# Recurrent cross-attention and a switch mixture of experts in fp32: each batch's x tokens go through one expert unsorted, with the contraction cut to 256 by states @ w1, and the states' tokens run in column groups of 32

## The chip, the cores and the metric

The kernel runs on one core of a Trainium2 chip. The metric is the time of one execution on the device, in microseconds (us); the median of a few runs is quoted, and one further execution is profiled. PE is TensorE (PEld its weight load), DVE VectorE, ACT ScalarE, POOL GpSimd; SP is the engine that here only issues DMAs.

## What is computed

There are B = 8 batches and H = 8 heads; x has S = 512 positions and state Ns = 32, both with D = 64 per head.

```python
scores = scale * x @ state.T;  a = softmax(scores)       # per batch and head
xread = a @ state                                         # 512 rows: the x tokens
scores2 = scale * state @ x.T; a2 = softmax(scores2)
sread = a2 @ x                                            # 32 rows: the states' tokens
x = concat([xread, sread]).transpose(0, 2, 1, 3).reshape(4352, 512)
logits = x @ w_gate;  expert_idx = argmax(logits);  gate_w = max of softmax(logits)
for e in range(8):                                        # w1[e] 512 x 1024, w2[e] 1024 x 512
    mask = expert_idx == e
    out[mask] = gate_w[mask] * (relu(x[mask] @ w1[e]) @ w2[e])
```

A batch contributes 512 x tokens and 32 states' tokens, 4096 and 256 in all. A row of xread is, head by head, a mixture of that batch's 32 states with the weights a. So for all x tokens of a batch x @ w1 = a @ (states @ w1), and the second form contracts over 8 heads x 32 states = 256 instead of over 512.

## The kernel before

All arithmetic of the heavy matmuls is fp32. The engines' orders come from a scheduler that moves instructions of the program as written; buffers come from rotating pools, so that a load waits until the last reader of its buffer is done.

*Attention*, one batch after another. `load_x` brings x in on SP (four DMAs of 256 KB a batch, three buffers); `transpose_x` turns it on PE through PSUM (`xT`, four copies by `evict`, which alternates between ACT and DVE); `prep_state` turns the states (`stT`) and multiplies them with the gate weights (`gst`, so that logits come from the weights a alone); `scores` puts the scores of four head pairs into `pc`, 64 output columns each, alternately in the lower and the upper half of the array. `read_weights` makes the softmax over the states on DVE (`sx`, in 32 x 32 transposes), with the exponential on ACT and the last multiplication on POOL, into `aT`. `write_weights`, `transpose_write` and `write_rows` do the same in the other direction (`a`, `a2T`, `pw`, `xs`) and write the states' tokens to DRAM (`st_dram`). `read_rows` multiplies the x tokens out (`px`, 256 columns a matmul), copies them into `row`, takes their logits (`pl`), and `route` chooses an expert and a slot for each token and scatters the rows, 128 at a time, to a buffer per expert in DRAM (`xs_dram`). `route_states` does this for 128 states' tokens read back from DRAM.

*Experts.* The tokens are sorted by expert, each expert's padded to tiles of T = 256; JT = 24 tiles always run. `fetch(j)` gathers a tile's rows on POOL and loads the 2 MB of `w1t` and the 2 MB of `w2t` on SP, two buffers each; `x_in` transposes the rows; `up` makes hT with K = 512 (64 records of 128 x 256 a tile), `down` multiplies by w2 with 512 columns a matmul (32 records), scales by the gate (L458) and scatters rows to the output on POOL (L459). Up, the next tile's transposes and down follow each other on PE.

Of the kernel before, what the change touches and what calls it, by code (L numbers as in the profile page):

```python
# [9 lines left out]
FP32 = mybir.dt.float32  # L10
# [18 lines left out]
):  # L29
    nc = tc.nc  # L30
# [32 lines left out]

# [11 lines left out]

# [3 lines left out]
    ebase = const.tile([128, E], FP32)  # L79
    nc.gpsimd.iota(ebase[:], pattern=[[NTOK, E]], base=0, channel_multiplier=0,  # L80
                   allow_small_or_imprecise_dtypes=True)
    base_e = const.tile([128, E], FP32)
    nc.vector.tensor_copy(out=base_e[:], in_=ebase[:])
    jio = const.tile([128, JT], FP32)
    nc.gpsimd.iota(jio[:], pattern=[[1, JT]], base=0, channel_multiplier=0,
                   allow_small_or_imprecise_dtypes=True)
    tri8 = const.tile([128, E, E], FP32)
    for e in range(E):
        nc.vector.tensor_scalar(tri8[:, e, :], rev8[:], float(E - e) - 0.5, None, ALU.is_ge)

# [10 lines left out]
    tok_s = const.tile([128, B // 4], I32)  # L101
    for g in range(B // 4):
        nc.vector.tensor_scalar(tmp_p[:], quad[:], float(SO - NS), iota_p[:, 0:1], ALU.mult, ALU.add)
        nc.vector.tensor_scalar(tok_s[:, g:g + 1], tmp_p[:], float(4 * g * SO + S), None, ALU.add)
# [4 lines left out]
    XB = 6  # L109

    xg_bufs = []
    for i in range(XB):
        xg = const.tile([128, XW], FP32, name=f"xg{i}")
        nc.gpsimd.memset(xg[:], 0.0)
        xg_bufs.append(xg)
# [25 lines left out]
    stT = att.tile([128, B, NPR, 2 * NS], FP32, bufs=1)  # L141
    gst = att.tile([128, B, 2, E], FP32, bufs=1)

# [22 lines left out]
    def transpose_x(b):  # L166
        xT = att.tile([128, NPR, NC, 128], FP32, tag="xT", name="xT")
        for j in range(NPR):
# [3 lines left out]
            evict(xT[:, j], pt[:])  # L172
# [10 lines left out]
    def read_weights(pc):  # L183
# [13 lines left out]
        aT = att.tile([128, 2, NC, 128], FP32, tag="aT", name="aT")  # L197
        nc.vector.transpose(aT[:].rearrange("p g c q -> p (g c q)"), sx[:].rearrange("p b n -> p (b n)"))
        return aT
# [15 lines left out]
    def transpose_write(a2):  # L215

        a2T = att.tile([128, 2, NC, 128], FP32, tag="a2T", name="a2T")
        for g in range(2):
# [90 lines left out]
    def route_states(g4):  # L309
# [4 lines left out]
        for c in range(NDC):  # L314
            nc.tensor.transpose(pt[:, c, :], srow[:, 0, ts(c, 128)], ident[:])
# [193 lines left out]
```

## Time and profile before

| what | us |
|---|---|
| median of 3 runs (898.52 to 899.72) | 899.61 |
| the profiled execution | 899.81 |
| its span, first to last instruction | 898.0 |
| PE busy (93% of the span) | 832.9 |
| DVE busy | 220.4 |
| ACT busy | 90.6 |
| POOL busy | 154.9 |

The profiled execution's time is 1.8 us more than its span. PE was granted 0.962 of its full clock in the mean. The DMA moved 138.03 MB.

### The profile page before, as it was taken

To read this page: it belongs to the slowest core of one execution; us is meant where nothing else is said; L and a number is where in the kernel's file an instruction comes from. 1 tells how busy PE (TensorE), PEld (TensorE's weight loads), DVE (VectorE), ACT (ScalarE), POOL (GpSimd) and SP (SyncE) were. 2 spreads that over 40 slices of the span, in tenths; PEclk is the share of its full clock that TensorE was granted. 3 is DMA by queue.
4 is the path that set the end of the run, shared out by engine and by line. 5 is a ranking of instruction groups with operands and counts; after the bars stand their busy time and mean duration, and the time that the engine had idled before them with its cause. 6 is when DMAs were issued, how large, how long until landed. Compare 5 with 4: busy or idle time off the path is not lost.

```text
span 898.0 us, 8743 instructions
## 1 busy us (share of the span) xinstructions
PE 832.9 (93%) x3452; PEld 565.0 (63%) x3452; DVE 220.4 (25%) x560; ACT 90.6 (10%) x176; POOL 154.9 (17%) x158
## 2 busy tenths in 40 slices
PE   3788898729999999999999999999999999999997
PEld 2375566617667766677666776667666776667764
DVE  4584878531111111111111111111111111111100
ACT  1232232201000000000000000000000000000000
POOL 3022324342001101111111101111011110100000
PEclk9888999666999999999999999999999999999999
DMA  9034542159545455463645536455364544445200
GB/s 164 1 74 121 132 125 93 67 175 386 182 161 203 147 205 176 175 213 112 229 152 210 178 129 227 147 199 162 137 205 159 202 124 162 156 160 199 97 1 0
DMA packets 86904, 138.03 MB, mean 154 GB/s; under 512 B 43214, under 2 KB 43214, under 8 KB 86864
## 3 DMA queue, kind: packets, MB, share of 16 engines
q1 hardware_dynamic: 70912, 109.06, 37.8%
q0 software_dynamic: 10400, 26.83, 7.8%
q10 hardware_dynamic: 5552, 1.59, 1.1%
q8 instruction: 27, 0.44, 0.2%
q14 instruction: 13, 0.11, 0.0%
HBM read 122.75 MB, written 22.05 MB: 161 GB/s over the span
## 4 chain that ended last, share of the span: by engine, by line
issue 65%; POOL 8%; DMA 2%; PE 2%; POOLq 1%; DVE 0%; DVEq 0%
POOL out_dram L459 5%; POOL xg L405 3%; PE ph L442 2%; DMA xg<-xs_dram,grow 1%; DMA w1t<-in_moe_w_dram 1%; POOLq L405 0%; POOLq L459 0%; POOLq L504 0%; DMA xs_dram<-srow,r_sli 0%; DVE ti L430 0%; DVE gw L432 0%; DVEq L430 0%
## 5 line engine op out<-in xcount | busy, mean ns | idle before, releaser
L442 PE MATMUL ph<-fxT,w1t 128*128 128x256 f32 x1536 | 338.4, 381 | 0.1
L455 PE MATMUL py<-w2t,hT 128*128 128x512 f32 x768 | 333.6, 592 | 0.0
L442 PEld LDWEIGHTS ph<-fxT,w1t 128*128 128x128 f32 x1536 | 293.8, 191 | 50.6 <-issue 11.4
L455 PEld LDWEIGHTS py<-w2t,hT 128*128 128x128 f32 x768 | 144.2, 190 | 172.3 <-issue 172.0
L459 POOL DMA_INDIRECT out_dram<-y,ti x48 | 48.4, 1009 | 357.0 <-DVE y L458 324.8
L458 DVE TENSOR_SCALAR y<-py,gw 128x512 f32<-128x512 f32 x48 | 36.1, 751 | 293.5 <-PE py L455 293.5
L405 POOL DMA_INDIRECT xg<-xs_dram,grow x48 | 49.5, 1032 | 247.7 <-PE ptx L427 235.0
L447 ACT ACTIVATE hT<-ph 128x512 f32<-128x512 f32 x48 | 28.7, 597 | 555.1 <-PE ph L442 555.1
L445 DVE TENSOR_SCALAR hT<-ph 128x512 f32<-128x512 f32 x48 | 33.1, 690 | 135.6 <-PE ph L442 135.4
L282 PE MATMUL px<-bd,aT 128*128 128x256 f32 x128 | 39.9, 439 | 11.6 <-DVE row L125 4.5
L430 DVE TENSOR_TENSOR ti<-xg,inv_i 128x1 int32<-128x1 int32 x48 | 6.0, 157 | 168.2 <-DMA out_dram<-y,ti 154.3
L268 POOL DMA_INDIRECT xs_dram<-row,r_sli x32 | 31.9, 996 | 60.2 <-DVE r_sli L265 25.1
L427 PE MATMUL ptx<-ident,xg 128*128 128x128 f32 x192 | 28.2, 290 | 13.8 <-DMA xg<-xs_dram,grow 13.7
L282 PEld LDWEIGHTS px<-bd,aT 128*128 128x128 f32 x128 | 24.4, 212 | 20.7 <-DVE row L125 6.5
L171 PE MATMUL pt<-ident,x_nat 128*128 128x128 f32 x128 | 26.4, 342 | 11.5 <-DMA x_nat<-in_x_dram 6.6
L427 PEld LDWEIGHTS ptx<-ident,xg 128*128 128x128 f32 x192 | 23.8, 149 | 17.9 <-issue 14.2
L171 PEld LDWEIGHTS pt<-ident,x_nat 128*128 128x128 f32 x128 | 18.7, 174 | 18.5 <-issue 7.2
L196 POOL TENSOR_TENSOR sx<-sx,sm 128x1024 f32<-128x1024 f32 x8 | 15.3, 1912 | 68.9 <-ACT xT L123 33.7
L179 PE MATMUL pc<-xT,stT 128*64 128x512 f32 x64 | 24.9, 705 | 0.0
L299 PE MATMUL pw<-x_nat,a2T 128*64 128x128 f32 x256 | 20.6, 318 | 3.1 <-DVE a2T L125 2.6
L123 ACT COPY fxT<-ptx 128x512 f32<-128x512 f32 x24 | 14.0, 585 | 88.9 <-PE ptx L427 86.0
L299 PEld LDWEIGHTS pw<-x_nat,a2T 128*64 128x64 f32 x256 | 17.8, 161 | 4.7 <-DVE a2T L125 2.9
(115 smaller groups left out, 331.4 us busy)
## 6 DMA issues: line engine op xcount, KB each, us to landing
w1t<-in_moe_w_dram SPq DMA_DIRECT2D x24, 2048.0 KB, 9.1
w2t<-in_moe_w_dram SPq DMA_DIRECT2D x24, 2048.0 KB, 10.0
x_nat<-in_x_dram SPq DMA_DIRECT2D x32, 256.0 KB, 4.8
xg<-xs_dram,grow POOLq DMA_INDIRECT x48, 6.9
out_dram<-y,ti POOLq DMA_INDIRECT x48, 3.2
bd<-in_state_dram ACTq DMA_DIRECT2D x8, 64.0 KB, 4.2
st_dram<-xs ACTq DMA_DIRECT2D x32, 16.0 KB, 3.5
xs_dram<-row,r_sli POOLq DMA_INDIRECT x32, 3.8
```

Of the source, the lines that this page charges most:

```text
L171: nc.tensor.transpose(pt[:, c, :], x_nat[b][:, c, ts(j, 2), :], ident[:])
L268: d = nc.gpsimd.indirect_dma_start(out=xs_dram[:], out_offset=bass.IndirectOffsetOnAxis(ap=sli[:, u:u + 1], axis=0), in_=row[:, u, :].bitc ...
L282: nc.tensor.matmul(px[:, ts(g, 256)], lhsT=aT[:, g, c, :], rhs=bd[:, b, g], start=True, stop=True, skip_group_check=True)
L299: nc.tensor.matmul(pw[ts(i, 64), g], lhsT=a2T[:, g, c, ts(i, 64)], rhs=x_nat[b][:, c, ts(2 * g + i, 2), :], start=(c == 0), stop=(c == NC ...
L405: nc.gpsimd.indirect_dma_start(out=xg_bufs[(NH * j + k) % XB][:].bitcast(I32), out_offset=None, in_=xs_dram[:], in_offset=bass.IndirectOff ...
L427: nc.tensor.transpose(pt[:, c, :], xg[:, ts(c, 128)], ident[:])
L442: nc.tensor.matmul(ph[:, i, :], lhsT=w1t[:, c, ts(2 * f2 + i, 128)], rhs=xT[:, c, :], start=(c == 0), stop=(c == NDC - 1), skip_group_chec ...
L445: nc.vector.tensor_scalar(hT[:, ts(f2, 2), :], ph[:], 0.0, None, ALU.max)
L447: nc.scalar.activation(hT[:, ts(f2, 2), :], ph[:], AF.Relu)
L455: nc.tensor.matmul(py[:], lhsT=hT[:, f, ts(k, 128)], rhs=w2t[:, f, :], start=(f == 0), stop=(f == NFC - 1))
L458: nc.vector.tensor_scalar(y[:], py[:], gw[:, k:k + 1], None, ALU.mult)
L459: d = nc.gpsimd.indirect_dma_start(out=out[:], out_offset=bass.IndirectOffsetOnAxis(ap=ti[:, k:k + 1], axis=0), in_=y[:], in_offset=None, ...
```

## The change

*Attention.* `read_rows` goes: x tokens are neither multiplied out nor sorted. What is kept of each batch are the weights `aT` and the states `stT`, for all batches. The copies of xT and of a2T are all ACT's. `logits_x` takes the logits of a batch; `route` works on many token groups at once (batches 0 and 1 after batch 1, all the rest at the end), and `choose` counts a batch's tokens per expert by a matmul with ones and takes the most frequent one as the batch's expert (`eb`). The first two batches' weights are loaded then. Only the states' tokens are sorted, into 16 groups of 32 that each belong to one expert (`ss_dram`, `eg`).

*Experts.* Per batch, `states_w1` multiplies the batch's 256 head-states by its expert's w1 into `G` (eight matmuls with 64 output columns); `up` multiplies G by aT with K = 256 and 512 columns; `down` is as before with 512 columns, and its rows go straight to the output by plain DMAs on SP. The states' tokens run in 4 rounds of four groups: the four groups of a round take 32 output columns each, with four experts' weights streamed past them, which `round_w1` and `round_w2` load in tiles of 1 MB, one DMA of 256 KB for each group, three buffers each. A round's up is laid between the column slices of an even batch's down, its down between those of the next batch's down. At the end, if any x token had another expert than its batch, a loop runs the pairs of batch and expert that are left.

```diff
-            evict(xT[:, j], pt[:])
+            nc.scalar.copy(xT[:, j], pt[:])
...
-            evict(a2T[:, g], pt[:])
+            nc.scalar.copy(a2T[:, g], pt[:])
...
-    def read_rows(b, aT):
...
-        for c in range(NC):
-            px = ps_o.tile([128, DM], FP32, tag="o", name="px")
-            for g in range(2):
-                nc.tensor.matmul(px[:, ts(g, 256)], lhsT=aT[:, g, c, :], rhs=bd[:, b, g],
-                                 start=True, stop=True, skip_group_check=True)
-            evict(row[:, c, 0:DM], px[:])
...
-        route(pl[:], row, tok_x[:, b, :], NC)
...
+    def logits_x(b):
+        pl = ps_s.tile([128, NC, E], FP32, tag="s", name="pl")
+        for c in range(NC):
+            for g in range(2):
+                nc.tensor.matmul(pl[:, c, :], lhsT=aT[:, b, g, ts(c, 128)], rhs=gst[:, b, g, :],
+                                 start=(g == 0), stop=(g == 1), skip_group_check=True)
+        evict(lg[:, ts(b, NC)], pl[:])
...
+    def choose(b0, nb):
...
+        for c in range(NC):
+            nc.tensor.matmul(pr[:], lhsT=ones_b[:], rhs=ohb[:, ds(b0, nb), c, :],
+                             start=(c == 0), stop=(c == NC - 1), skip_group_check=True)
...
+    def expert_of(table, i, engines=(SP,)):
...
+    def load_w1(b, e):
+        w1s[b] = wpool.tile([128, NDC, F], FP32, tag="w1", name="w1t")
+        nc.sync.dma_start(out=w1s[b][:], in_=moe_w1[ds(e, 1)].rearrange("o (c p) f -> p (o c) f", p=128))
+
+    def load_w2(b, e):
+        w2s[b] = wpool.tile([128, NFC, DM], FP32, tag="w2", bufs=2, name="w2t")
+        nc.sync.dma_start(out=w2s[b][:], in_=moe_w2[ds(e, 1)].rearrange("o (c p) f -> p (o c) f", p=128))
 
     def weights(b):
         xT = transpose_x(b)
...
     for b in range(B):
-        aT, (a2, s2) = soft
+        a2, s2 = soft
         if b + 2 < B:
             load_x(b + 2)
         if b + 1 < B:
             soft = weights(b + 1)
         a2T = transpose_write(a2)
         write_rows(b, a2T, s2)
-        read_rows(b, aT)
-        if b == 5:
-            route_states(0)
-    route_states(1)
...
+        logits_x(b)
+        if b == 1:
+            route(0, 2 * NC)
+            choose(0, 2)
+            for i in range(2):
+                e = expert_of(eb, i)
+                if i == 0:
+                    load_w1(0, e)
+                load_w2(i, e)
+    logits_s()
+    route(2 * NC, (B - 2) * NC + NST)
+    choose(2, B - 2)
...
+    left = const.tile([128, 1], FP32)
+    nc.vector.tensor_reduce(left[:], cmx[:, :, 0], AX.X, ALU.add)
+    left_i = const.tile([128, 1], I32)
+    nc.vector.tensor_scalar(left_i[:], left[:], -1.0, float(B * S), ALU.mult, ALU.add)
...
+    def states_w1(w1t, st):
+
+        G = ffn.tile([128, 2, F], FP32, tag="G", bufs=1, name="G")
+        for g in range(2):
+            for k in range(2):
+                pg = ps_h.tile([128, 512], FP32, tag="h", name="pG")
+                for i in range(2):
+                    j = 2 * g + i
+                    nc.tensor.matmul(pg[ts(i, 64), :], lhsT=st[:, j, :], rhs=w1t[:, j, ts(k, 512)],
+                                     start=True, stop=True, skip_group_check=True)
+                evict(G[:, g, ts(k, 512)], pg[:])
+        return G
+
+    def up(G, a, insert=None):
+        hT = [ffn.tile([128, S], FP32, tag="hT", bufs=12, name="hT") for _ in range(NFC)]
+        for f in range(NFC):
+            ph = ps_h.tile([128, S], FP32, tag="h", name="ph")
+            for g in range(2):
+                nc.tensor.matmul(ph[:], lhsT=G[:, g, ts(f, 128)], rhs=a[:, g, :],
+                                 start=(g == 0), stop=(g == 1))
+            relu(hT[f][:], ph[:])
...
+    def down(hT, w2t, store, insert=None):
+        for c in range(NC):
+            py = ps_y.tile([128, DM], FP32, tag="y", name="py")
+            for f in range(NFC):
+                nc.tensor.matmul(py[:], lhsT=hT[f][:, ts(c, 128)], rhs=w2t[:, f, :],
+                                 start=(f == 0), stop=(f == NFC - 1))
+            store(c, py)
+            if insert:
+                insert(c)
...
+    def store_batch(b):
+        rows = out[ds(b * SO, S)].rearrange("(p c) f -> p c f", c=NC)
...
+        def store(c, py):
+            y = ffn.tile([128, DM], FP32, tag="y", bufs=3, name="y")
+            scaled(y[:], py[:], gw[:, NC * b + c, :])
+            no_dep(nc.sync.dma_start(out=rows[:, c], in_=y[:]))
+        return store
...
+    def round_in(r):
+        xg = ffn.tile([128, XW], FP32, tag="xg", name="xg")
+        nc.sync.dma_start(out=xg[:].bitcast(I32), in_=ss_dram[ts(r, 128)])
+        rd[r].update(xg=xg, e=[expert_of(eg, 4 * r + q) for q in range(4)])
...
+    def round_w1(r, k, half):
+        t = ffn.tile([128, 4, 512], FP32, tag="s1", bufs=3, name="s1")
+        for q in range(4):
+            nc.sync.dma_start(out=t[:, q], in_=moe_w1[ds(rd[r]["e"][q], 1), ts(k, 128), ts(half, 512)]
+                              .rearrange("o p f -> p (o f)"))
+        rd[r][1, k, half] = t
...
+    def round_w2(r, f):
+        t = ffn.tile([128, 4, DM], FP32, tag="s2", bufs=3, name="s2")
+        for q in range(4):
+            nc.sync.dma_start(out=t[:, q], in_=moe_w2[ds(rd[r]["e"][q], 1), ts(f, 128), :]
+                              .rearrange("o p f -> p (o f)"))
...
+    def round_x(r):
+        pt = ps_t.tile([128, NDC, 128], FP32, tag="t", name="ptx")
+        for c in range(NDC):
+            nc.tensor.transpose(pt[:, c, :], rd[r]["xg"][:, ts(c, 128)], ident[:])
+        xT = ffn.tile([128, NDC, 128], FP32, tag="sxT", name="sxT")
+        evict(xT[:], pt[:])
...
+    def round_up(r, k):
+        for half in range(2):
+            for q in range(4):
+                nc.tensor.matmul(rd[r]["ph"][half][ts(q, 32), :], lhsT=rd[r]["xT"][:, k, ts(q, 32)],
+                                 rhs=rd[r][1, k, half][:, q, :], start=(k == 0), stop=(k == NDC - 1),
...
+    def round_h(r):
+        h = ffn.tile([128, F], FP32, tag="sh", bufs=1, name="sh")
+        for half in range(2):
+            relu(h[:, ts(half, 512)], rd[r]["ph"][half][:])
...
+        for u in range(2):
+            pt = ps_t.tile([128, 4, 128], FP32, tag="t", name="pth")
+            for i in range(4):
+                nc.tensor.transpose(pt[:, i, :], h[:, ts(4 * u + i, 128)], ident[:])
+            evict(hT[:, ts(u, 4)], pt[:])
...
+    def round_down(r, f):
+        for q in range(4):
+            nc.tensor.matmul(rd[r]["py"][ts(q, 32), :], lhsT=rd[r]["hT"][:, f, ts(q, 32)],
+                             rhs=rd[r][2, f][:, q, :], start=(f == 0), stop=(f == NFC - 1),
...
+    def round_out(r):
+        xg = rd[r]["xg"]
+        y = ffn.tile([128, DM], FP32, tag="y", bufs=3, name="ys")
+        scaled(y[:], rd[r]["py"][:], xg[:, DM:DM + 1])
+        no_dep(nc.gpsimd.indirect_dma_start(
...
+
+    G = states_w1(w1s[0], stT[:, 0])
+    e_next = expert_of(eb, 1)
+    load_w1(1, e_next)
+    round_in(0)
+    hT = up(G, aT[:, 0])
+    for b in range(B):
+        r = b // 2
+        if b % 2 == 0:
+            round_x(r)
+            for k in range(NDC):
+                for half in range(2):
+                    round_w1(r, k, half)
+        else:
+            round_h(r)
+            for f in range(NFC):
+                round_w2(r, f)
+            if r + 1 < NR:
+                round_in(r + 1)
+        if b + 1 < B:
+            G = states_w1(w1s[b + 1], stT[:, b + 1])
+        if b + 2 < B:
+            e = expert_of(eb, b + 2)
+            load_w1(b + 2, e)
+            load_w2(b + 2, e)
+
+        def insert(c):
+            if b % 2 == 0:
+                round_up(r, c)
...
-    def down(j):
...
-        for k in range(NH):
-            py = ps_o.tile([128, DM], FP32, tag="o", name="py")
-            for f in range(NFC):
-                nc.tensor.matmul(py[:], lhsT=hT[:, f, ts(k, 128)], rhs=w2t[:, f, :],
-                                 start=(f == 0), stop=(f == NFC - 1))
...
+                round_down(r, 2 * c)
+                round_down(r, 2 * c + 1)
+        down(hT, w2s[b], store_batch(b), insert)
+        if b % 2:
+            round_out(r)
+        if b + 1 < B:
+            hT = up(G, aT[:, b + 1])
...
+    n_left = nc.values_load(left_i[0:1, 0:1], min_val=0, max_val=B * S,
+                            skip_runtime_bounds_check_because="a count of tokens")
+    with tc.If(n_left > 0):
```

PE in the expert stage before, one tile after another: ph is up, ptx the transposes, py down.

```order
L442 MATMUL ph<-fxT,w1t 128x256 x32
L427 MATMUL ptx<-ident,xg_111 128x128 x4
L427 MATMUL ptx<-ident,xg_113 128x128 x4
L455 MATMUL py<-w2t,hT 128x512 x16
L442 MATMUL ph<-fxT,w1t 128x256 x32
```

Here only the next tile's transposes stand between up and down.

PE in the changed kernel, from up of a batch to the middle of its down, in a batch that carries a round's up (pG is states_w1 of the next batch, pgh the round, the names with s_ its weight tiles).

```order
L460 MATMUL ph<-aT,G 128x512 x16
L511 MATMUL ptx<-ident,xg 128x128 x4
L450 MATMUL pG<-w1t,stT 64x512 x8
L471 MATMUL py<-w2t,hT 128x512 x8
L520 MATMUL pgh<-s_1723,sxT 32x512 x4
L520 MATMUL pgh<-s_1728,sxT 32x512 x4
L471 MATMUL py<-w2t,hT 128x512 x8
L520 MATMUL pgh<-s_1733,sxT 32x512 x4
L520 MATMUL pgh<-s_1738,sxT 32x512 x4
```

Two weight tiles of the round now stand in PE's line between each two column slices of down.

SP before, one tile's weights.

```order
L410 TENSOR_LOAD eidx
L414 ISA
L414 DMA w1t<-in_moe_w_dram 128x4x1024
L416 ISA
L416 DMA w2t<-in_moe_w_dram 128x8x512
```

Nothing else stands in that line between one tile and the next.

SP in the changed kernel, from the second half of a round's last up tile (L497) to the first down tile (L504); L483 stores a column slice of the output.

```order
L497 ISA
L497 DMA s_1345<-in_moe_w_dram 128x512
L497 ISA
L497 DMA s_1345<-in_moe_w_dram 128x512
L310 TENSOR_LOAD eb
L319 ISA
L319 DMA w1t<-in_moe_w_dram 128x4x1024
L323 ISA
L323 DMA w2t<-in_moe_w_dram 128x8x512
L483 DMA out_dram<-y 128x512
L504 ISA
L504 DMA s_1511<-in_moe_w_dram 128x512
```

The loads of the batch after next, a store and the tiles of a round now stand in one line on SP, each behind the wait of the one ahead.

PE in the changed kernel at the end of attention: a_1009 is the last batch's a, pls the states' logits.

```order
L227 MATMUL pt<-ident,a_1009 128x128 x8
L450 MATMUL pG<-w1t,stT 64x512
L238 MATMUL pw<-x_nat,a2T 64x128 x8
L263 MATMUL pt<-ident,srow 128x128 x4
L450 MATMUL pG<-w1t,stT 64x512 x4
L238 MATMUL pw<-x_nat,a2T 64x128 x8
L252 MATMUL pl<-gst,aT 128x8 x8
L450 MATMUL pG<-w1t,stT 64x512
L267 MATMUL pls<-wg,sT 128x8 x4
L263 MATMUL pt<-ident,srow 128x128 x4
L267 MATMUL pls<-wg,sT 128x8 x4
```

Six of the first batch's eight states_w1 matmuls have moved ahead of the states' logits; the other two and the first up stand behind them and behind the counts that follow.

## Rows read from the trace of the kernel before

**Rows 1.** Busy time by stage: us, engine busy (instructions), granted clock, DMA share, GB/s.
```profile
28.60:154.10 125.50, 104.16 (x726) 75.30 (x727) 90.98 (x223) 37.57 (x83) 35.62 (x30) 0.90 0.36 92
154.10:190.10 36.00, 25.90 (x178) 19.96 (x178) 18.00 (x62) 6.86 (x15) 12.53 (x12) 0.79 0.30 100
190.10:210.10 20.00, 6.11 (x23) 3.91 (x24) 8.04 (x48) 1.17 (x2) 11.43 (x12) 0.50 0.75 277
210.10:893.10 683.00, 682.93 (x2475) 457.32 (x2475) 91.43 (x202) 41.53 (x70) 86.54 (x85) 1.00 0.48 166
893.10:898.00 4.90, 0.00 (x0) 0.00 (x0) 0.73 (x1) 0.00 (x0) 0.98 (x1) 0.71 0.01 0
```

**Rows 2.** PE's timeline over one tile: start us, us, instruction, count.
```profile
410.57 13.98 PE L442 MATMUL ph<-fxT,w1t 128*128 128x256 f32 x64
424.38 1.04 PE L427 MATMUL ptx<-ident,xg 128*128 128x128 f32 x8
425.26 13.90 PE L455 MATMUL py<-w2t,hT 128*128 128x512 f32 x32
439.00 6.21 PE L442 MATMUL ph<-fxT,w1t 128*128 128x256 f32 x28
```

**Rows 3.** Groups by shape: count | busy us, mean ns | idle before, releaser.
```profile
L442 PE MATMUL ph<-fxT,w1t 128*128 128x256 f32 x1536 | 338.4, 381 | 0.1
L455 PE MATMUL py<-w2t,hT 128*128 128x512 f32 x768 | 333.6, 592 | 0.0
L123 ACT COPY xT<-pt 128x512 f32<-128x512 f32 x16 | 9.4, 585 | 50.1 <-PE pt L171 47.3 <-DVE xT L125 2.8
```

**Rows 4.** PE's timeline in attention, 64 and 128 output columns.
```profile
105.65 1.97 PE L299 MATMUL pw<-x_nat,a2T 128*64 128x128 f32 x32 [1.37 <-DVE a2T L125]
115.78 1.13 PE L282 MATMUL px<-bd,aT 128*128 128x256 f32 x4
116.97 1.06 PE L179 MATMUL pc<-xT,stT 128*64 128x512 f32 x4
117.87 0.59 PE L179 MATMUL pc<-xT,stT 128*64 128x512 f32 x1
```

**Rows 5.** The instructions on sx (min/median/max, first and last start), DVE's timeline.
```profile
L187 DVE STREAM_TRANSPOSE sx<-pc x8: 1218/1250/1251, 28.6 to 154.1; 128x1024 f32<-128x1024 f32 x8
...
101.44 1.25 DVE L187 STREAM_TRANSPOSE sx<-pc 128x1024 f32<-128x1024 f32 x1 [1.41 <-PE pc L179]
110.62 0.69 DVE L125 COPY row<-px 128x512 f32<-128x512 f32 x1
112.03 1.25 DVE L198 STREAM_TRANSPOSE aT<-sx 128x1024 f32<-128x1024 f32 x1 [0.72 <-POOL sx L196]
118.93 1.25 DVE L187 STREAM_TRANSPOSE sx<-pc 128x1024 f32<-128x1024 f32 x1 [1.58 <-PE pc L179]
```

**Rows 6.** Timeline from the last batch's xs to the first up.
```profile
178.33 0.61 DVE L304 TENSOR_SCALAR xs<-pw,s 128x128 f32<-128x128 f32 x2 [3.31 <-PE pw L299]
186.41 0.65 PE L315 MATMUL pt<-ident,srow 128*128 128x128 f32 x4 [0.59 <-DMA srow<-st_dram]
190.14 0.19 PE L251 MATMUL pr<-r_oh,U 128*128 128x8 bf16 x1 [1.06 <-DVE r_oh L238]
203.01 3.37 PE L427 MATMUL ptx<-ident,xg 128*128 128x128 f32 x12 [12.66 <-DMA xg<-xs_dram,grow]
210.12 16.90 PE L442 MATMUL ph<-fxT,w1t 128*128 128x256 f32 x64
```

**Rows 7.** DMA issues: KB each, median us from issue to landing.
```profile
w2t<-in_moe_w_dram SPq DMA_DIRECT2D x24, 2048.0 KB, 10.0
x_nat<-in_x_dram SPq DMA_DIRECT2D x32, 256.0 KB, 4.8
```

**Rows 8.** Busy time while x loads, and while one w2t loads.
```profile
3.00:13.00 10.00, 4.69 (x16) 3.04 (x16) 7.80 (x20) 1.17 (x2) 5.39 (x6) 1.00 1.38 220
245.00:249.00 4.00, 4.00 (x20) 3.51 (x19) 0.00 (x0) 0.00 (x0) 0.00 (x0) 1.00 1.02 392
```

More of the change, by code (lines that the diff above doesn't have):

```diff
@@ L16 @@
 SP = mybir.EngineType.SP
+DVE = mybir.EngineType.DVE
 @with_exitstack
@@ new lines, in logits_s @@
+    def logits_s():
+        sT = att.tile([128, NST, NDC, 128], FP32, tag="sT", bufs=1, name="sT")
+        pl = ps_s.tile([128, NST, E], FP32, tag="s", name="pls")
+        for t in range(NST):
+            nc.sync.dma_start(out=srow[:, t, 0:DM], in_=st_dram[ts(t, 128)])
+            pt = ps_m.tile([128, NDC, 128], FP32, tag="m", name="pt")
+            for c in range(NDC):
+                nc.tensor.transpose(pt[:, c, :], srow[:, t, ts(c, 128)], ident[:])
+            evict(sT[:, t], pt[:])
+        for t in range(NST):
+            for c in range(NDC):
+                nc.tensor.matmul(pl[:, t, :], lhsT=sT[:, t, c, :], rhs=wg[:, c, :],
+                                 start=(c == 0), stop=(c == NDC - 1), skip_group_check=True)
+        evict(lg[:, NX:], pl[:])
@@ new lines @@
+    nc.vector.tensor_copy(out=srow[:, :, DM:DM + 1], in_=gw[:, NX:])
+    nc.vector.tensor_copy(out=srow[:, :, DM + 1:DM + 2].bitcast(I32), in_=tok_s[:].unsqueeze(2))
+    for t in range(NST):
+        d = nc.gpsimd.indirect_dma_start(
+            out=ss_dram[:], out_offset=bass.IndirectOffsetOnAxis(ap=slot_i[:, t:t + 1], axis=0),
+            in_=srow[:, t, :].bitcast(I32), in_offset=None,
+            bounds_check=NG * 32 - 1, oob_is_err=False,
+        )
+        tc.declare_no_dep(d.ins, group="scatter", reason="every token has a row of its own")
+        tc.add_to_no_dep_group("scatter", d.ins)
@@ L466, with no_dep @@
-    fetch(0)
-    fetch(1)
-    x_in(0)
-    for j in range(JT):
-        up(j)
-        if j + 1 < JT:
-            x_in(j + 1)
-        down(j)
-        if j + 2 < JT:
-            fetch(j + 2)
-    for pool in (ps_s, ps_o, ps_m, ffn):
+    ps_h = tc.alloc_tile_pool(name="ps_h", bufs=3, space=PSUM)
+    ps_y = tc.alloc_tile_pool(name="ps_y", bufs=2, space=PSUM)
+    ps_g = tc.alloc_tile_pool(name="ps_g", bufs=2, space=PSUM)
+    ps_t = tc.alloc_tile_pool(name="ps_t", bufs=1, space=PSUM)
+    def no_dep(d):
+        tc.declare_no_dep(d.ins, group="y", reason="every row of the result is written once")
+        tc.add_to_no_dep_group("y", d.ins)
@@ new lines @@
+    rd = [dict() for _ in range(NR)]
+    def round_in(r):
[8 more added lines that the diff above has]
+        rd[r][1, k, half] = t
@@ L478 @@
+    for pool in (ps_t, ps_g, ps_y, ps_h, ffn):
         pool.release()
```

382 lines of the change are left out of this document (190 added, 192 removed).

## The prediction

> **What bounds the kernel now.** I read the stages first [rows 1]: busy time of each engine between five marks, with TensorE's granted clock and what the DMA moved. Attention runs to 154 us with no engine full. 36 us follow in which the last batch is routed, then 20 us in which PE works 6, then 683 us in which PE works 682.93 at the full clock (1.00, the 2.4 GHz level) and the DMA is busy 0.48 of the time. So the kernel is its expert stage, and that stage is PE. One tile of 256 tokens shows its cadence [rows 2]: from start to start, up takes 13.8 us, eight transposes 0.9, down 13.7: 28.43 us from up to up, and 24 times 28.43 = 682. Nothing waits there, so PE time saved there is saved in the end.
>
> The prices [rows 3]: one fp32 matmul of 512 columns is two records, 333.6 / 768 = 0.434 us each, so 0.869 a matmul. A 256-column record is 338.4 / 1536 = 0.220. By rows through the array both cost the same.
>
> **What the expert stage becomes.** With the reference's inputs each batch's 512 x tokens all have their largest logit at one expert (the smallest lead over the second is 0.00024), so one pass per batch does all of them, the count of left tokens is 0, and the block under tc.If is branched over. Of the states' 256 tokens the experts get 32, 120, 0, 29, 1, 40, 0 and 34: 11 groups of 32. But the program always runs 16 groups, 4 rounds; this doesn't depend on data.
>
> Up: K is 256 instead of 512 (two matmuls of 512 columns per slice of F, 16 a batch): 8 x 16 x 0.869 = 111.2 us. Down is as before per token: 8 x 32 x 0.869 = 222.4. Before these two were 338.4 + 333.6 for 24 x 256 = 6144 rows, half again as many as there are x tokens: the padding to tiles goes too.
>
> New, states_w1: eight matmuls of 64 output columns, alternating between the halves of the array. Do they overlap? Scores have this form, and there four records of 512 columns took 1.06 us [rows 4], against 4 x 0.434 = 1.74 in a row: two at a time (0.87 and the modelled end). The 32 pw records of 128 columns took 1.97, little over half of the 3.5 that they need one after another at half a 256-column record. The px records beside them, 128 output columns wide, show no overlap: four of 256 columns in 1.13. So states_w1 costs 4 x 0.869 = 3.5 a batch; the first lies ahead of the stage, 7 x 3.5 = 24.3.
>
> New, rounds: a round is 32 matmuls up and 32 down, each 32 output columns and 512 streamed, in turn over the four column groups. No row before has 32 columns. Bounds: as one column group of 128 (no overlap), 4 x 64 x 0.869 = 222.4; two at a time as the scores, 111.2; four at a time, 55.6. I take four at a time: in the scores the two records that ran together belonged to different groups, and their own group alone held back the next, so each group has its own line; the row nearest says that the number of groups sets the factor.
> The Trainium skill, "TensorE: Matmul & The Clock Gate", section "Part 3: Packing small matmuls", gives 2.38x for three column tiles, not 3x; an estimate from it for four is 1.3 to 1.35 durations a pack, some 18 us more than the 55.6. No run here shows it.
>
> Transposes are 4 x 12 of 128 columns at 0.88 / 8 = 0.11 [rows 2]: 5, with their ends 6. For the ten changes of form a batch (128, 64 and 32 columns) no row stands: nothing, or the tail of a record, 0.59 - 0.43 = 0.16 [rows 4], if the array empties; I take 0.1 each: 8. Sum 111.2 + 222.4 + 24.3 + 55.6 + 6 + 8 = 427.5, and 2.9 for the start: the first up took 16.9 instead of 14.0 [rows 6], after 20 us at clock 0.50 (the 1.2 GHz level) [rows 1], and PE will have idled again.
>
> Hidden work: an eviction of 512 columns (ACT 0.585, DVE 0.69) has 1.74 us a slice of up with two engines in turn. Stores wait on SP behind loads, but each frees a y buffer three slices later, 6.95 us apart.
>
> **Do the weights come in time?** A round's half needs eight tiles of 1 MB, each four DMAs of 256 KB; three buffers. Tile 3 is issued when its buffer is read (after the first column slice of down) and is wanted a slice later: 6.95 + 1.74 = 8.7 us. So are tiles 5 and 7. On SP the next w1 and w2 stand behind tile 7, and w2 waits for the end of down besides; w1 has over 10 us to spare and w2 a whole batch. Bounds for a tile: 256 KB x loads landed 4.8 us after issue, a whole 2 MB w2t 10.0 [rows 7]. A tile is half a w2t in bytes and 2 KB runs, so I take 6: no wait. At 10.0 each would be 1.3 late. In bytes: a pair of batches moves 27 MB in 107 us, 255 GB/s; w2t's 2 KB runs moved 392 once started, x's 256-byte runs 220 [rows 8].
> The Trainium skill, "DMA: Bandwidth & Descriptors", section "Rules for kernel authors", wants 1 MiB or more per DMA, against this change's 256 loads of 256 KB; by the fit of its "Anatomy of one DMA" (for the other issue path) an estimate is 2.6 us a load, 666 us if one waited for another. The x loads agree on latency, not on waiting: 220 GB/s is one each 1.2 us.
>
> **Attention.** Gone are the px matmuls, the row copies and their 32 scatters, and a route per batch. The batch from 101.44 to 118.93 took 17.5, mean 125.5 / 7 = 17.9 [rows 5], and DVE sets it (copies stand between softmax steps). Five copies of 0.68 a batch leave DVE, two for good and three to ACT: 3.4 if all were on the chain, nothing if none. ACT takes three at 0.585 and has room (38 of 125 us busy). I take 2.9: 14.6 a batch. Against it two one-off delays, 3 each: route and choose for batches 0 and 1 stand in the middle (DVE some 15 small ones, PE waiting), and x of batch 5 queues on SP behind 6.3 MB of weights, 16 us at 392. 7 x 14.6 + 6 = 108.2 instead of 125.5; the first sx stays at 28.6.
>
> After the last sx PE must still do the states' logits before up. Before: 36 to pr, 20 more to the first up, of which 12.7 wait for the gathers [rows 6]. After: to the end of aT 11.4 (11.8 in the batch of rows 5), xs 0.7, from xs through DRAM to the transpose 7.5 (178.9 to 186.4), to pr 3.7 and 1.3 for wider operations, then two states_w1 pairs: 27. No gather: weights were loaded in batch 3, the scatter of 256 rows and its load end under the first up.
>
> **Sum.** 28.6 + 108.2 + 27 + 427.5 + 2.9, the end 4.9 as before [rows 1] and 2 for the branch: 601.1. The profiled execution is 899.81 for a span of 898.0, so 1.8 more: 602.9. It lies 0.2 over the median, so 603.
>
> **Rivals.**
> 1. The groups share something and a pack takes longer: between the 1.97 / 1.75 = 1.13 of pw [rows 4] and rival 2's 2.0 I take a third, 55.6 + 18, 621. For: pw is over half. The Trainium skill's section on packing points here.
> 2. Only two groups at a time: + 55.6, 659. For: two is all that the trace shows.
> 3. No overlap: + 166.8, 770. Against: rows 4.
> 4. Tiles late: three a batch by 1.3 us, 24 x 1.3 = 31, 634; the DMA at x's 220 GB/s would give 500 us for 109 MB instead of 427, 676.
> 5. Attention keeps its 17.9: + 17, 620.
> 6. Slower than before: SP's loads of 256 KB go one after another, 256 x 4.8 = 1229 us where PE has 428. It decides from 2.8 us a load (898 - 164 - 7 = 727 over 256). Against: 220 GB/s for the x loads.
>
> **How the numbers follow.** Forecast 0.48, rival 1 0.16, rival 2 0.14, rival 3 0.04, rival 4 0.10, rival 5 0.06, rival 6 0.02. All but the last are faster. 588 (attention at 13 a batch) to 680 leaves out rivals 3 and 6 and the ends of others. Under 0.2% is about what a measurement of this kernel cannot tell from no change: same 0.01, slower 0.02, faster 0.97.
>
> **What would show it.** Four round matmuls in about 0.87 us (1.74: rival 2; 3.5: rival 3); up 13.9, down 27.8 less rounds; up to up some 53.5 a batch; PE without idle time from the first up; tiles landing within 8.7 us; the first up near 164; sx every 14.6; no instruction of the loop. Wrong it would be if PE waits for s1 or s2 tiles in the middle of down, or if the clock falls within the rounds.

## The result and the profile after

The median is 603.25 us (601.86 to 604.14, 4 runs) against 899.66 (898.52 to 900.83) for the kernel before: a ratio of 0.6704, 95% interval 0.6688 to 0.6719. The profiled execution took 603.11, its span is 601.3 us, PE is busy 544.4 us of it (91%), and the DMA moved 122.63 MB.

The stages of the changed kernel, with marks at the first and the last sx, at the first up and near the end (columns as in [rows 1]):

```profile
0.00:23.70 23.70, 10.22 (x39) 6.12 (x40) 4.86 (x13) 3.96 (x7) 5.55 (x16) 1.00 0.87 200
23.70:133.10 109.40, 80.30 (x596) 56.22 (x597) 63.98 (x118) 41.58 (x90) 13.38 (x7) 0.83 0.40 112
133.10:164.47 31.37, 22.28 (x157) 15.27 (x157) 15.95 (x49) 5.97 (x13) 1.91 (x1) 0.71 0.06 14
164.47:596.00 431.53, 431.53 (x1442) 170.41 (x1440) 52.70 (x77) 45.67 (x74) 5.07 (x5) 1.00 0.71 243
596.00:601.30 5.30, 0.06 (x4) 0.00 (x0) 0.00 (x0) 0.69 (x1) 0.98 (x1) 0.89 0.15 51
```

The expert stage fell from 683 to 431.5 us, and PE has no idle time in it: 431.53 busy of 431.53, at the full clock. Attention between the first and the last sx fell from 125.5 to 109.4 only, with PE's granted clock at 0.83 where it was 0.90 [rows 1]. From the last sx to the first up it takes 31.4 us where it took 56.

The sx of the changed kernel one by one, on DVE's timeline:

```profile
23.70 1.25 DVE L195 STREAM_TRANSPOSE sx<-pc 128x1024 f32<-128x1024 f32 x1 [3.98 <-PE pc L187]
31.52 1.25 DVE L195 STREAM_TRANSPOSE sx<-pc 128x1024 f32<-128x1024 f32 x1 [0.42 <-PE pc L187]
45.93 1.23 DVE L195 STREAM_TRANSPOSE sx<-pc 128x1024 f32<-128x1024 f32 x1
...
97.03 1.25 DVE L195 STREAM_TRANSPOSE sx<-pc 128x1024 f32<-128x1024 f32 x1 [0.78 <-PE pc L187]
...
133.10 1.25 DVE L195 STREAM_TRANSPOSE sx<-pc 128x1024 f32<-128x1024 f32 x1 [1.45 <-PE pc L187]
```

and the third of the kernel before:

```profile
56.25 1.25 DVE L187 STREAM_TRANSPOSE sx<-pc 128x1024 f32<-128x1024 f32 x1 [0.58 <-PE pc L179]
```

The mean interval is 15.6 us, but the batches differ: the first two intervals are 7.8 and 14.4, the last five 17.4 in the mean (45.93 to 133.10). In the kernel before, the last five were 19.6 in the mean (56.25 to 154.1 [rows 5]).

PE's timeline over the first batch of the expert stage (as [rows 2]): ph is up, pG states_w1, py down, pgh the round.

```profile
164.47 15.08 PE L460 MATMUL ph<-aT,G 128*128 128x512 f32 x32
179.39 0.60 PE L511 MATMUL ptx<-ident,xg 128*128 128x128 f32 x4
179.92 3.65 PE L450 MATMUL pG<-w1t,stT 128*64 128x512 f32 x16
183.50 7.13 PE L471 MATMUL py<-w2t,hT 128*128 128x512 f32 x16
190.56 1.93 PE L520 MATMUL pgh<-s,sxT 128*32 128x512 f32 x16
192.42 7.13 PE L471 MATMUL py<-w2t,hT 128*128 128x512 f32 x16
...
219.17 14.00 PE L460 MATMUL ph<-aT,G 128*128 128x512 f32 x32
233.01 0.60 PE L532 MATMUL pth<-ident,sh 128*128 128x128 f32 x4
```

From start to start, a set of 16 records with 32 output columns takes 1.86 us (190.56 to 192.42). One after another they would take 16 x 0.434 = 6.94, so four groups do run at once. A slice of down takes 7.06, which is 16 x 0.434 and 0.12.

The groups by shape, to be held against [rows 3]:

```profile
L471 PE MATMUL py<-w2t,hT 128*128 128x512 f32 x512 | 228.4, 599 | 0.0
L460 PE MATMUL ph<-aT,G 128*128 128x512 f32 x256 | 113.1, 600 | 0.0
L450 PE MATMUL pG<-w1t,stT 128*64 128x512 f32 x128 | 35.7, 625 | 1.6 <-ACT G L125 1.6
L520 PE MATMUL pgh<-s,sxT 128*32 128x512 f32 x256 | 30.8, 598 | 0.0
L538 PE MATMUL pgy<-s,shT 128*32 128x512 f32 x256 | 30.8, 598 | 0.0
```

Up went from 338.4 to 113.1: two thirds of the rows (no padding, and the states' tokens go in the rounds) by half the contraction. Down went from 333.6 to 228.4, by the rows alone. States_w1 and the rounds give 97 of this 330 back.

### The profile page after: what moved, and what is told of

Its sections match the earlier page's. It is cut to its first block, busy times and chain, and to the rows that moved or that the text cites. A ratio compares the mean times of both kernels' runs of the same rounds, so it can differ in the third digit from the quotient of the medians.

```text
span 601.3 us, 6244 instructions
## 1 busy us (share of the span) xinstructions
PE 544.4 (91%) x2229; PEld 248.0 (41%) x2229; DVE 137.5 (23%) x255; ACT 97.9 (16%) x185; POOL 26.9 (4%) x30
## 2 busy tenths in 40 slices
DMA packets 94513, 122.63 MB, mean 204 GB/s; under 512 B 43791, under 2 KB 43791, under 8 KB 94480
## 4 chain that ended last, share of the span: by engine, by line
issue 54%; PE 30%; DVE 6%; DMA 3%; POOL 2%; ACT 2%; ACTq 1%; SPq 0%; POOLq 0%
PE py L471 9%; PE ph L460 5%; PE pc L187 4%; PE pG L450 2%; PE pw L238 2%; PE pl L252 2%; POOL sx L204 2%; DMA bd<-in_state_dram 1%; PE pgy L538 1%; ACTq L245 1%; PE pgh L520 1%; DVE aT L205 1%; PE pt L227 1%; DVE sm L201 1%; PE pg L170 1%
## 5 line engine op out<-in xcount | busy, mean ns | idle before, releaser
L471 PE MATMUL py<-w2t,hT 128*128 128x512 f32 x512 | 228.4, 599 | 0.0
L471 PEld LDWEIGHTS py<-w2t,hT 128*128 128x128 f32 x512 | 94.7, 190 | 132.4 <-issue 132.4
L460 PE MATMUL ph<-aT,G 128*128 128x512 f32 x256 | 113.1, 600 | 0.0
L460 PEld LDWEIGHTS ph<-aT,G 128*128 128x128 f32 x256 | 48.5, 192 | 65.4 <-issue 59.0
L438 DVE TENSOR_SCALAR y<-py,gw 128x512 f32<-128x512 f32 x16 | 12.0, 750 | 258.4 <-PE py L471 241.3
L436 ACT ACTIVATE y<-py,gw 128x512 f32<-128x512 f32 x16 | 11.0, 687 | 195.3 <-PE py L471 195.3
L450 PE MATMUL pG<-w1t,stT 128*64 128x512 f32 x128 | 35.7, 625 | 1.6 <-ACT G L125 1.6
L520 PE MATMUL pgh<-s,sxT 128*32 128x512 f32 x256 | 30.8, 598 | 0.0
L538 PE MATMUL pgy<-s,shT 128*32 128x512 f32 x256 | 30.8, 598 | 0.0
L179 PEld LDWEIGHTS pt<-ident,x_nat 128*128 128x128 f32 x128 | 15.6, 155 | 18.3 <-ACT xT L180 9.0
L180 ACT COPY xT<-pt 128x512 f32<-128x512 f32 x32 | 17.5, 590 | 24.1 <-PE pt L179 14.0
L164 PE MATMUL pt<-ident,bd 128*128 128x128 f32 x32 | 7.1, 360 | 13.9 <-DMA bd<-in_state_dram 7.6
L170 PE MATMUL pg<-wg,stT 128*64 128x8 f32 x64 | 7.0, 248 | 13.0 <-DVE stT L127 12.7
L450 PEld LDWEIGHTS pG<-w1t,stT 128*64 128x64 f32 x128 | 9.4, 140 | 16.2 <-issue 14.2
```

What stands on the lines that cost most here:

```text
L179: nc.tensor.transpose(pt[:, c, :], x_nat[b][:, c, ts(j, 2), :], ident[:])
L180: nc.scalar.copy(xT[:, j], pt[:])
L450: nc.tensor.matmul(pg[ts(i, 64), :], lhsT=st[:, j, :], rhs=w1t[:, j, ts(k, 512)], start=True, stop=True, skip_group_check=True)
L460: nc.tensor.matmul(ph[:], lhsT=G[:, g, ts(f, 128)], rhs=a[:, g, :], start=(g == 0), stop=(g == 1))
L471: nc.tensor.matmul(py[:], lhsT=hT[f][:, ts(c, 128)], rhs=w2t[:, f, :], start=(f == 0), stop=(f == NFC - 1))
L520: nc.tensor.matmul(rd[r]["ph"][half][ts(q, 32), :], lhsT=rd[r]["xT"][:, k, ts(q, 32)], rhs=rd[r][1, k, half][:, q, :], start=(k == 0), sto ...
```

## The experiments

Each is compared with the changed kernel's 603.25; the runs of the kernel before beside them had medians of 899.3 to 901.5. Edits are shown against the changed kernel.

### Two column groups, and one

```diff
-  rd[r]["ph"][half][ts(q, 32), :]
+  rd[r]["ph"][half][ts(2 * (k % 2) + q % 2, 32), :]
```

The rest of the call is left out here; its start and stop flags follow the index. With one group the index is `ts(k, 32)`; the round's down is edited likewise.

> The four matmuls of a weight tile write two column groups of 32 in turn instead of four (which pair changes from slice to slice), so the states' rows are not the reference's; count, shape and loads are the same. Theory (each column group is a line of its own, so the number of groups sets the factor): eight matmuls, 16 records of 0.434 us, take 16 x 0.434 / 2 + 0.12 = 3.6 us instead of 1.86; there are 32 such sets, + 32 x 1.74 = 55.5, so 659 us. Rival (a record with 32 output columns is quicker by itself, wherever it stands): 1.86 as before, 603 us.

> As the run with two groups, but all four matmuls of a tile write one column group, another one in each slice; the states' rows are not the reference's. Theory (a line for each group): 16 records one after another, 16 x 0.434 + 0.12 = 7.06 us a set instead of 1.86, + 32 x 5.2 = 166, 770 us. Rival (a 32-column record is quicker by itself): 603 us; a mixture of both would lie between.

Measured: 657.4 us (656.09 and 658.72) and 767.1 (765.85 and 768.42). PE's timeline with two groups:

```profile
188.84 3.63 PE L520 MATMUL pgh<-s,sxT 128*32 128x512 f32 x16
192.40 7.13 PE L471 MATMUL py<-w2t,hT 128*128 128x512 f32 x16
```

and with one:

```profile
191.46 7.05 PE L520 MATMUL pgh<-s,sxT 128*32 128x512 f32 x16
198.44 7.13 PE L471 MATMUL py<-w2t,hT 128*128 128x512 f32 x16
```

A set takes 1.86 us with four groups, 3.56 with two, 6.98 with one: 16 x 0.434 divided by the number of groups, and 0.04 to 0.12. So the groups are lines of their own, and four of them share nothing that costs time beyond these 0.12 us a set. The Trainium skill, "TensorE: Matmul & The Clock Gate", section "Part 3: Packing small matmuls", gives 2.38x for three column tiles. No run here has three; four gave 6.98 / 1.86 = 3.75x, or 1.86 / 1.74 = 1.07 durations where the prediction's estimate from that figure was 1.3 to 1.35, and the measurement decides.

### The weight tiles: two buffers, or none to load

```diff
-        t = ffn.tile([128, 4, 512], FP32, tag="s1", bufs=3, name="s1")
+        t = ffn.tile([128, 4, 512], FP32, tag="s1", bufs=2, name="s1")
```

and the same for s2; with resident tiles (w1's part; w2's is alike, and `kept` starts as an empty dictionary):

```diff
+        if "w1" in kept:
+            rd[r][1, k, half] = kept["w1"]
+            return
-        t = ffn.tile([128, 4, 512], FP32, tag="s1", bufs=3, name="s1")
+        kept["w1"] = t = ffn.tile([128, 4, 512], FP32, tag="s1", bufs=1, name="s1")
```

> The round's weight tiles rotate in two buffers instead of three. A tile of the next slice is then issued when the set before has read its buffer, 8.0 us before it is wanted (a column slice of down, 7.06, and half a set, 0.93) instead of a tile earlier. Theory (the third buffer only adds slack: a load of 256 KB lands 5.0 us after issue, and SP issues the eight of two tiles in 4.45 us, which fits into 8.0 by less than 1 us): 603 to 606 us. Rival (SP's line with its waits for stores and for w2 between the tiles, or the transfers, already use the slack): tiles late by 1 us or more in 24 of the 32 sets, 627 us or more, with idle time of PE ahead of the rounds that ends on a DMA.

> Only the first w1 tile and the first w2 tile of the rounds are loaded, and every round reads these two; the other 62 MB of tiles are not loaded, so the states' rows are not the reference's. Theory (the tiles' transfers are hidden whole and disturb nothing): 603 us, and the sets of a round still take 1.86. Rival (the transfers take something from PE's reads, which is the 0.11 to 0.12 by which each slice of down and each set is longer than its records of 0.434): 64 such pieces by 0.11 = 7 us less, 596 us.

Measured: 614.85 us (613.10 to 618.11) with two buffers, 602.21 (601.93 to 603.84) with resident tiles. The second moves 57.55 MB instead of 122.63; its range lies within that of the changed kernel, and its sets and slices take what they took, as the counterpart of the set at 190.56 shows:

```profile
191.30 1.92 PE L527 MATMUL pgh<-s,sxT 128*32 128x512 f32 x16
```

So the tiles' transfers cost nothing as they stand, and the 0.12 a piece is not theirs. With two buffers, SP's timeline shows why the slack was needed:

```profile
190.35 0.35 SPq L483 DMA_DIRECT2D out_dram<-y  x1
190.97 4.10 SPq L497 DMA_DIRECT2D s<-in_moe_w_dram  x8
```

and PE's the set that waits for these loads:

```profile
191.39 7.13 PE L471 MATMUL py<-w2t,hT 128*128 128x512 f32 x16
198.45 3.08 PE L520 MATMUL pgh<-s,sxT 128*32 128x512 f32 x16
201.47 7.13 PE L471 MATMUL py<-w2t,hT 128*128 128x512 f32 x16
```

SP needs 4.1 us to issue eight loads, about half a microsecond each. The last lands some 5 us after it is issued, near 200, and the second tile of the set is wanted at 199.4. The set takes 3.02 instead of 1.86. In this trace 15 of the 32 sets take longer than 1.86, by 0.1 to 1.5 us each and 12.7 together. My theory here was wrong by counting issue and landing side by side instead of one after the other; the rival had the place right and its price, at least 24, too high: 11.6. With three buffers one of the two tiles is issued a slice earlier, and this is hidden. The Trainium skill, "DMA: Bandwidth & Descriptors", section "Rules for kernel authors", wants 1 MiB or more per DMA for the greatest bandwidth; the resident tiles show that 256 loads of a quarter of that cost nothing here while they are hidden.

### The copies on ACT undone

```diff
-            nc.scalar.copy(xT[:, j], pt[:])
+            evict(xT[:, j], pt[:])
...
-            nc.scalar.copy(a2T[:, g], pt[:])
+            evict(a2T[:, g], pt[:])
```

> One part of the change undone: the copies of xT and of a2T alternate between ACT and DVE again, as before. Theory by the prediction's term (copies stand in DVE's line between softmax steps, five of 0.68 us a batch were worth 2.9, three of them went to ACT): 3/5 of 2.9 by 7 batches, + 12, 615 us. Theory after reading the trace (DVE is idle for 9 of the 18 us of a batch, and two xT copies of 0.54 us on ACT stand ahead of the exponential for which DVE waits 2.16): what DVE takes over lies in its idle time, and the time is 603 within 4 us.

Measured: 605.83 us (604.50 to 608.38), 2.6 more, as the second theory had it. Its sx:

```profile
L195 DVE STREAM_TRANSPOSE sx<-pc x8: 1249/1249/1250, 24.2 to 139.3; 128x1024 f32<-128x1024 f32 x8
```

From the first to the last it takes 115.1 us instead of 109.4, with the granted clock at 0.76 instead of 0.83; the first up comes 29.4 after the last sx instead of 31.4. So the prediction's term for these three copies, 12, was too large by some 6 in that stretch and by some 9 in the whole. That the rest lies in DVE's idle time, as the second theory says, is not shown by itself, since the clock changed too.

### What ties one batch of attention to the next

The timeline of all engines between two batches of the changed kernel, from POOL's multiplication to the next sx:

```profile
107.31 1.91 POOL L204 TENSOR_TENSOR sx<-sx,sm 128x1024 f32<-128x1024 f32 x1 [14.62 <-DVE sm L203]
109.25 1.25 DVE L205 STREAM_TRANSPOSE aT<-sx 128x1024 f32<-128x1024 f32 x1 [2.09 <-POOL sx L204]
110.42 0.25 DVE L127 COPY stT<-pt 128x128 f32<-128x128 f32 x1
...
111.18 1.09 PE L187 MATMUL pc<-xT,stT 128*64 128x512 f32 x1
...
111.47 3.65 PE L187 MATMUL pc<-xT,stT 128*64 128x512 f32 x7
...
115.16 1.25 DVE L195 STREAM_TRANSPOSE sx<-pc 128x1024 f32<-128x1024 f32 x1 [1.79 <-PE pc L187]
```

The copy into stT, which the next batch's scores need, stands on DVE behind aT of this batch. So the softmax of one batch and the scores of the next follow each other instead of overlapping: 18.1 us from the sx at 97.03 to that at 115.16. And the eight records of the scores take 3.9 us, which at the full clock took 1.06 for four [rows 4]. The grouped row of the scores says how often, as min / median / max in ns, first for the kernel before and then for the changed one:

```profile
L179 PE MATMUL pc<-xT,stT x64: 592/593/1115, 24.9 to 153.5; 128*64 128x512 f32 x64
L187 PE MATMUL pc<-xT,stT x64: 592/1060/1095, 19.9 to 132.4; 128*64 128x512 f32 x64
```

Two runs test the two causes. One turns the states earlier:

```diff
     load_x(1)
+    prep_state(0)
+    prep_state(1)
     soft = weights(0)
...
         xT = transpose_x(b)
-        prep_state(b)
...
             soft = weights(b + 1)
+        if b + 2 < B:
+            prep_state(b + 2)
```

The other adds six matmuls of no use ahead of the scores:

```diff
         pc = ps_c.tile([128, 2, S], FP32, tag="c", name="pc")
+        for k in range(6 if b > 1 else 0):
+            nc.tensor.matmul(pc[:, k % 2, :], lhsT=ident[:], rhs=xT[:, k % NPR],
+                             start=True, stop=True, skip_group_check=True)
```

> The states of a batch are turned one batch earlier, so that the copies into stT no longer stand on DVE behind the last step of the batch before (the transpose into aT). Theory (this copy ties two batches together: aT of batch b, then stT 0.25, gate products, scores 4.4 us at half clock, then sx of batch b + 1): sx of the next batch follows aT at once, every 13.7 us instead of up to 18.1, the last sx some 12 us earlier, 591 us. Rival (PE's clock alone is what attention lost, or the xT copies on ACT hold the scores back as well): sx stays at 15.6 in the mean, 603 us.

> In batches 2 to 7 six further fp32 matmuls of 512 columns stand on PE between the transposes of x and the scores; they write pc before the scores overwrite it and change no result. Theory (with px gone PE idles more, its granted clock in attention is 0.83 instead of 0.90, the scores' eight records take 3.5 us instead of 1.8 and lie on the chain): the clock is 1.00 again, the scores take 1.8, six batches by 1.7 us, 593 us. Rival (the added 6 x 0.87 = 5.2 us stand in the chain themselves, or the clock stays down and they take 10.4): slower, 603 + 6 x 3 = 621 us or more.

Early states: 596.25 us (595.39 to 597.22). The sx:

```profile
L195 DVE STREAM_TRANSPOSE sx<-pc x8: 1249/1250/1251, 28.6 to 127.7; 128x1024 f32<-128x1024 f32 x8
```

The mean interval fell from 15.6 to 14.2, and the first sx came at 28.6 because both batches' states now stood ahead of it, so that the last one is 5.4 us earlier. From the fourth sx on DVE still waits for the scores, 1.9 to 3.2 us a batch. The tie was real: the intervals are 10 us shorter together, and the scores stayed just behind. The scores' median record fell as well, from 1.06 to 0.67 us, so a part of the 10 may be the clock's; it isn't told apart.

Busy PE: 614.31 us (612.75 to 615.54), slower. The timeline of PE in one batch:

```profile
119.92 2.84 PE L187 MATMUL pc<-xT,ident 128*128 128x512 f32 x6
122.69 1.94 PE L190 MATMUL pc<-xT,stT 128*64 128x512 f32 x8
```

Here the granted clock of attention was 0.97, and the scores took 1.94 where they had taken 3.9: with the added records ahead of them they ran at the 2.4 GHz level. But 2.8 us of the added records stand in the chain themselves, more than the 1.7 that the clock gave. What the clock alone is worth stays unpriced.

### Attention, the route, and both

SP issues the states' tokens' stores instead of ACT, where the four issues of a batch took 2.5 us; states are early from batch 2 on. The rest of the store's call is left out.

```diff
-        prep_state(b)
+        if b < 2:
+            prep_state(b)
...
             soft = weights(b + 1)
+        if b + 2 < B:
+            prep_state(b + 2)
...
-            nc.scalar.dma_start(out=st_dram
+            nc.sync.dma_start(out=st_dram
```

> Two edits in attention. From batch 2 on the states are turned one batch earlier (batches 0 and 1 as in the change, since turning both first put the first sx at 28.6 in the run with early states), and the four small DMAs a batch that write the states' tokens are issued by SP instead of ACT. Theory (the copy into stT ties batches together, 4.4 us a batch, and then the xT copies that stand behind 2.5 us of DMA issue on ACT hold the scores, for which DVE still waited 2.0 to 3.2): the first sx at 23.7 again, sx every 13 us from batch 2 on, the last sx at 118 instead of 133.1, 588 us. Rival (the issues on ACT are not what holds the xT copies; the clock and PSUM buffers are): sx every 14.3 as in the run with early states, the last sx near 123, 593 us.

Measured: 584.77 us (583.24 to 586.22).

```profile
L195 DVE STREAM_TRANSPOSE sx<-pc x8: 1206/1250/1251, 23.7 to 119.5; 128x1024 f32<-128x1024 f32 x8
```

The first sx at 23.7, the last at 119.5 instead of 133.1; intervals of 7.6 to 20.3, mean 13.7. It moves two things at once, so the share of the issues on ACT isn't shown apart.

The end of attention in the changed kernel, ACT's timeline, at the copy that holds the last two matmuls of states_w1 and so the first up:

```profile
161.92 0.58 ACT L125 COPY G<-pG 128x512 f32<-128x512 f32 x1 [3.04 <-DVE cum L381]
```

The copies into G wait for the route (cum is one of its last steps), though nothing in G comes from it; G lies in a pool that is allocated when attention's pool, which the route still uses, is released (that this is the reason was not tried by itself). A version that allocates the second stage's pools ahead of the route and puts logits, route and counts inside the first up, here its core:

```diff
-    logits_s()
-    route(2 * NC, (B - 2) * NC + NST)
-    choose(2, B - 2)
...
     G = states_w1(w1s[0], stT[:, 0])
+    read_states()
...
-    hT = up(G, aT[:, 0])
+    hT = up(G, aT[:, 0], states_in)
...
+            if b == 0 and c < 2:
+                if c == 1:
+                    round_x(0)
+                    round_up(0, 0)
+                    round_up(0, 1)
```

In `states_in` the transposes of the states' tokens follow the fourth and fifth slice of up, and logits, route and counts the sixth.

> The first up no longer waits for the states' logits, the route of batches 2 to 7 and the counts: these stand inside the first up, after its fourth to sixth slice (with the transposes and the first round's two first slices of batch 0 taken together after the second column slice of down). Theory (of the 31.4 us from the last sx to the first up only the end of aT and states_w1 is needed by it): the first up starts near 150 instead of 164.5 and grows by about 3 us of small matmuls, 592 us. Rival (the round's tokens and tiles come through DRAM after the counts, 20 us from the counts to xg in place): PE waits for xg in the first down, 3 to 6 us back, 596 us; if PE waits for the read-back states' rows inside up as long as before it, 603.

Measured: 601.28 us (599.83 to 602.19). The first up did start at 153.45 instead of 164.47, but the second at 218.16 instead of 219.17: 10 of 11 us were given back. Up stretched from 14.9 to 18.5 with the small matmuls inside, and the first down stretched from 35.7 to 42.5, since two sets stood together with three tile buffers. PE's timeline there, where the first 24 records take 5.11 instead of 2.8 us:

```profile
189.52 0.60 PE L459 MATMUL ptx<-ident,xg 128*128 128x128 f32 x4
189.96 1.02 PE L419 MATMUL py<-w2t,hT 128*128 128x512 f32 x2
190.91 5.11 PE L468 MATMUL pgh<-s,sxT 128*32 128x512 f32 x24
```

Both together, with the first round spread out again:

```diff
             if b == 0:
+                if c == 1:
+                    round_x(0)
+                if c:
+                    round_up(0, c - 1)
...
+            def last_slice(f):
+                if b == 0 and f == 3:
+                    round_up(0, 3)
-            hT = up(G, aT[:, b + 1])
+            hT = up(G, aT[:, b + 1], last_slice)
```

> The two edits in attention of the run beside it, and the route of batches 2 to 7 inside the first up as in the run with the late route, but with the first round's four pieces of up one slice later each (after the second, third and fourth column slice of the first down and inside the second up), so that they never need more than two weight tiles at once. Theory (the late route won 11 us at the first up, and lost 7 in the first down because two sets stood together with three buffers): what the run beside it gives, less 10 to 12 for the route, near 577 us. Rival (the small matmuls of the route cost their 4 us inside up and the loads through DRAM hold the first down in any case): 5 less than the run beside it at most, 583 us.

Measured: 577.30 us (576.88 to 578.62), ratio to before 0.6416 (0.6404 to 0.6428): it beats both kernels, 7.5 less than the run with attention alone, between the 10 to 12 of the theory and the 5 of the rival. With three of its four sets, spread out, the first down took 35.9 us instead of 42.5. From the last sx to the first up it takes 16.6 us instead of 31.4 (117.12 to 133.67).

The last run spreads the first weights' loads:

```diff
-                if i == 0:
-                    load_w1(0, e)
-                load_w2(i, e)
+        if b == 2:
+            load_w1(0, expert_of(eb, 0))
+        if b == 3:
+            load_w2(0, expert_of(eb, 0))
+        if b == 5:
+            load_w2(1, expert_of(eb, 1))
```

> As the run with all edits, but the first weights (6.3 MB) are not loaded together after batch 1: w1 of batch 0 is loaded after batch 2, its w2 after batch 3, the w2 of batch 1 after batch 5. Theory (one burst of 6.3 MB on SP's line, 70 to 87 us, delays the next x and with it the scores: sx came after 13.8 and 21.2 us there, and after 12.4 to 15 elsewhere): both intervals shrink to 14, last sx at 109 instead of 117.1, 569 us. Rival (the long interval is the half clock and the order on PE, not the transfer): last sx at 115 or later, 575 to 577 us.

Measured: 576.72 us (575.38 to 578.30), no difference from the run with both (577.30), and the last sx at 115.6: the theory fell, and the rival's numbers held. PE's timeline in the interval of 20.4 us that stayed:

```profile
91.11 2.79 PE L252 MATMUL pl<-gst,aT 128*128 128x8 f32 x16 [1.88 <-ACT gst L125]
93.75 1.95 PE L179 MATMUL pt<-ident,x_nat 128*128 128x128 f32 x8
```

The next batch's transposes stand on PE behind the logits pl, and these wait for a copy of gst, at half clock. That this order is the whole of the interval wasn't tried.

## Why the prediction was right, and which of its errors cancelled

The sum of its terms, against the same pieces of the profiled execution:

| term | predicted | measured |
|---|---|---|
| first sx | 28.6 | 23.7 |
| seven batches to the last sx | 108.2 | 109.4 |
| last sx to the first up | 27 | 31.4 |
| half-clock start of the first up | 2.9 | 1.1 |
| expert stage | 427.5 | 430.5 |
| end and branch | 6.9 | 5.2 |
| span | 601.1 | 601.3 |

- **The expert stage**, 72% of the time, was right in mechanism and size. Up 13.84 a batch (13.9), four matmuls of a round 0.93 with half of the 0.12 that a set has over its records (0.87), and no stall. Ten changes of form a batch at 0.1 had been an assumption; each slice of down and each set measured 0.12 over its records, 7.7 us in all where 8 were predicted. That the change of form is what costs them was not tried by itself. Rivals 1 to 3 fall by the set's 1.86 and by the two runs with fewer groups, which came out at 657.4 and 767.1 where rivals 2 and 3 had been priced at 659 and 770. The 3 us that are missing are in states_w1, 4.6 instead of 3.5 where the round's transposes cut it in two, and in transposes.
- **The tiles** came in time: a load landed after 5.0 us in the median, where the prediction took 6 for a tile. It left out SP's issue time, half a microsecond each; with two buffers this would have decided. Rivals 4 and 6 fall by the resident tiles' 602.2.
- **Attention** was mis-sized in steps that cancel, and that the sum came out so near is luck. The first sx did not stay at 28.6: the states reach PE at 18 us in both kernels, but before, 15 transposes of the next batch's x stood on PE from there to the first scores at 24.9, and now 2 stand there and the scores start at 19.9. The 108.2 were 14.6 a batch and two delays of 3, or 15.5 in the mean, and 15.6 was measured; but 14.6 was not the cadence. The last five intervals were 17.4 in the mean, near rival 5's 17.9, none of them (15.2 to 18.1) stands out as delayed, and the short first two made up for them. Two things were wrong in the 14.6: the three copies a batch that ACT took were worth 2.6 us in all and not 12, and the clock fell from 0.90 to 0.83, so that the scores, on the chain, took 3.6 to 4.0 us instead of 1.9 in four of the seven later batches. A lower clock was looked for within the rounds, not here. "27" measured 31.4: the counts (pr) came 26.9 us after the last sx and not 24.6, and from there it took 4.4 instead of 2; the last copies into G stood behind the route.
- With the first sx at 28.6 the measured rest would have given 608; the range held that too.

## What to carry to other kernels

Small outputs can share the array: put independent matmuls of 32 output columns in four column groups in turn. Here the time was little over that of a quarter of the records, with each group's weights in time and a third buffer to cover issue and landing. When the bound engine's stage shrinks, read the stage ahead of it anew: here its clock fell after work was taken off PE, and the chain through DVE, ACT and the scores stayed nearly as long as it was. And look for false ties: a copy in an engine's line behind another batch's last step cost more here (7.0 us) than the copies moved to ACT were worth (2.6). Memory that is shared with a stage that is not yet done may be another; its price was not measured by itself.

## What the runs showed that I had not expected

A set costs only 0.12 us above an ideal quarter with four groups (1.86 against 6.98 / 4 = 1.74) and 0.07 with two (3.56 against 3.49). Removing PE work from attention was followed by a rise of the scores' median record from 0.59 to 1.06 us, the 1.2 GHz level, and adding work that is of no use brought 0.59 back. SP's issue of a load whose address holds an expert's number took half a microsecond (eight in 4.1 us), more than PE needs for one record of 512 columns (0.434).
